# Moving two small shift terms behind the sums of the next row tiles on VectorE, in the first norm

## The chip, the cores and the metric

The kernel runs on one core of a Trainium2 chip. The metric is the device time of one execution in microseconds (us); lower is better. A difference counts as one only above 2%. Engines as the profile names them: PE is TensorE (PEld its weight loads), DVE is VectorE, ACT is ScalarE, POOL is GpSimd, SP issues the loads.

## The reference, cut to what matters

```python
def reference(A_x, A_wqkv, A_wo, B_x, B_w_gate, B_w_up, B_w_down, c, w_mod):
    x = A_x                                            # 1 x 2048 x 1024, bf16
    mod = (silu(c) @ w_mod).reshape(1, 6, 1, 1024)     # sa, ca, ga, sb, cb, gb
    h = layernorm(x) * (1 + ca) + sa                   # the first norm: this case
    x = x + ga * linear_attention(h, A_wqkv, A_wo)
    h = layernorm(x) * (1 + cb) + sb
    return x + gb * swiglu(h, B_w_gate, B_w_up, B_w_down)
```

The change touches `layernorm(x)` for the first four row tiles of 128 rows, so the first 12 us of the kernel. Everything behind is the same in both kernels.

## The kernel before: the parts that matter

Nothing large can start on TensorE until four row tiles are loaded, normalised and transposed. The work is split over all engines. VectorE sums tiles 0, 2 and 3 (two half-sums `bn_stats` and a `bn_aggr` each); ScalarE sums tile 1; POOL computes `rstd` as a power. Tiles 0 and 1 are normalised by ScalarE as `x * rstd + shift`; VectorE forms the shift (`NMR`, a 128x1 value, minus mean times rstd). Tiles 2 and 3 are normalised by VectorE itself. TensorE meanwhile runs dummy matmuls (`warm`), then transposes each tile.

In the traces below VectorE starts its instructions in the order of the program. The loads of x are issued first, one tile each, on one queue:

```python
for st in range(4):
    P.dma("x0_%d" % st, XRES[:, st, :], xv[:, st, :])
# ... then the loads of w_mod and wqkv, in the order of their use

s0_, s2_, s3_ = ln1_stats_ops(0), ln1_stats_ops(2), ln1_stats_ops(3)   # bn_stats, bn_stats, bn_aggr

def act_xn(st, mean):
    P.dve("tensor_scalar", out=NMR[:, st:st + 1], in0=mean, scalar1=RSTD[:, st:st + 1],
          scalar2=-1.0, op0=ALU.mult, op1=ALU.mult)                    # the shift term
    P.act("activation", out=XRES[:, st, :], in_=XRES[:, st, :],
          func=ACT.Identity, scale=RSTD[:, st:st + 1], bias=NMR[:, st:st + 1])

warm(13, bank=3)                 # TensorE: 13 dummies
act_stats(1)                     # ScalarE: sums of tile 1
for f in s0_:
    f()
ln1_rstd1(0)                     # epsilon on VectorE, power on POOL
s2_[0]()
act_xn(0, MV[:, 0, 0:1])
s2_[1]()
tile_transposes(0)
warm(5, bank=3)                  # TensorE: 5 more dummies
act_var(1)
s2_[2]()
P.dve("tensor_scalar", out=VE[:, 2:3], in0=MV[:, 2, 1:2], scalar1=EPS, scalar2=None, op0=ALU.add)
P.pool("tensor_tensor", out=RSTD[:, 1:3], in0=VE[:, 1:3], in1=NEGHALF[:, 0:2], op=ALU.pow)
s3_[0]()
s3_[1]()
act_xn(1, SUMX[:, 1:2])
s3_[2]()
ln1_rstd1(3)
ln1_xn(2)
tile_transposes(2)
mod_sc(WCA, 8, range(2))         # TensorE: first scale columns of the modulation
ln1_xn(3)
fin_ca(0, 2)
tile_transposes(1, 3)
# ... cut: the projection (q_phase_chunk0), which starts with HT[0] and WQK[0]
```

## Time and profile before

| | before |
|---|---|
| time, median of 3 runs | 831.08 us (830.88 to 831.48) |
| span of the profiled execution | 829.0 us |
| TensorE busy | 819.6 us, 99% |
| first weight load of the projection | 11.96 us |

The profile's page of the kernel before, from its parts 1 (busy us of each engine, share of the span, instructions) and 4 (the chain of work that ended last, by engine):

```profile
PE 819.6 (99%) x4005; PEld 379.2 (46%) x4083; DVE 312.5 (38%) x665; ACT 197.5 (24%) x336; POOL 40.4 (5%) x57
...
PE 97%; DVE 2%; issue 1%; ACT 0%; DVEq 0%; ACTq 0%
```

TensorE bounds the kernel, so only time in which TensorE waits in the head, or arrives late there, can matter. The page also counts 4005 matmuls against 4083 weight loads: 78 matmul records are missing from this trace.

The timeline of VectorE in the kernel before (start in us, length in us, instruction, out<-in, count, idle time before it and what ended it):

```profile
5.33 0.69 DVE L176 BATCH_NORM_STATS2 stats<-xres 128x6 f32<-128x512 bf16 x1
6.18 0.21 DVE L176 TENSOR_SCALAR nmr<-mv,rstd 128x1 f32<-128x1 f32 x1 [0.16 <-POOL rstd L176]
6.31 0.68 DVE L176 BATCH_NORM_STATS2 stats<-xres 128x6 f32<-128x512 bf16 x1
6.91 0.20 DVE L176 SCALAR_TENSOR_TENSOR mv<-sumx,sumsq 128x1 f32<-128x1 f32 x1
...
8.71 0.20 DVE L176 TENSOR_SCALAR nmr<-sumx,rstd 128x1 f32<-128x1 f32 x1
8.83 0.21 DVE L176 BATCH_NORM_AGGREGATE mv<-stats 128x2 f32<-128x12 f32 x1
...
10.13 0.55 DVE L176 TENSOR_SCALAR xres<-xres,mv,rstd 128x1024 bf16<-128x1024 bf16 x1 [0.45 <-POOL rstd L176]
```

The two `nmr` lines are the shift terms. The first waits 0.16 us for POOL between the two half-sums of tile 2: that is the wait which the change wants to fill.

ScalarE in the same profile (the `xres` lines normalise tiles 0 and 1):

```profile
6.49 0.19 ACT L176 ACTIVATION_READ_ACCUMULATOR ht<-xres 128x1 f32 x1
6.58 1.23 ACT L176 ACTIVATE xres<-xres,nmr,rstd 128x1024 bf16<-128x1024 bf16 x1
9.01 1.24 ACT L176 ACTIVATE xres<-xres,nmr,rstd 128x1024 bf16<-128x1024 bf16 x1 [1.20 <-DVE nmr L176]
```

And TensorE: transposes of tile 0, five dummies, transposes of tile 2, and those of tiles 1 and 3 (16):

```profile
8.04 0.61 PE L176 MATMUL ps<-ident,xres 128*128 128x128 bf16 x8
8.48 1.24 PE L176 MATMUL ps<-e,ident 128*128 128x512 bf16 x5
9.74 0.62 PE L176 MATMUL ps<-ident,xres 128*128 128x128 bf16 x8
...
10.60 1.15 PE L176 MATMUL ps<-ident,xres 128*128 128x128 bf16 x16
```

### The profile page before, as it was taken

What the parts mean: (1) busy time and instruction counts of PE and PEld (TensorE: products, weight loads), DVE (VectorE), ACT (ScalarE), POOL (GpSimd) and SP (SyncE); (2) the same over time, 40 slices, a digit from 0 to 9 for tenths busy, and PEclk for the clock granted to TensorE, in tenths of its full rate; (3) what the DMA queues carried; (4) which work ended last, traced back from release to release, by engine and by line L of the source; (5) the groups of instructions that cost most, each with busy time, mean ns of one, the idle gap of its engine ahead of it and who ended that gap; (6) DMA issues with size and microseconds to landing.
All of it is one profiled execution on the core that took longest, in us unless ns stands there. A gap on an engine that the chain in (4) does not pass through costs nothing.

```text
span 829.0 us, 9939 instructions
## 1 busy us (share of the span) xinstructions
PE 819.6 (99%) x4005; PEld 379.2 (46%) x4083; DVE 312.5 (38%) x665; ACT 197.5 (24%) x336; POOL 40.4 (5%) x57
## 2 busy tenths in 40 slices
PE   8999999999999999999999999999999999999998
PEld 4544444454444444444444444444444444444444
DVE  5797986756955521121221112122111111221111
ACT  4757641323242111011111101111110111111011
POOL 1010000000130000030000003000000300000000
PEclk9999999999999999999999999999999999999999
DMA  9969655928397995700455571045557004553000
GB/s 320 291 151 232 149 155 172 202 103 304 63 255 231 292 252 153 189 25 18 123 153 154 150 184 33 18 124 153 154 150 189 26 19 123 152 154 86 0 26 26
DMA packets 199245, 119.28 MB, mean 144 GB/s; under 512 B 57880, under 2 KB 182944, under 8 KB 199200
## 3 DMA queue, kind: packets, MB, share of 16 engines
q1 hardware_dynamic: 199184, 118.65, 52.8%
q8 instruction: 32, 0.52, 0.3%
q14 instruction: 13, 0.11, 0.0%
q10 hardware_dynamic: 16, 0.00, 0.0%
HBM read 100.67 MB, written 4.33 MB: 127 GB/s over the span
## 4 chain that ended last, share of the span: by engine, by line
PE 97%; DVE 2%; issue 1%; ACT 0%; DVEq 0%; ACTq 0%
PE ps L176 97%; DVE acc L176 1%; DVE pkt L176 0%; DVE e L176 0%; DVE pqt L176 0%; DVE ht L176 0%; DVE mask L176 0%; ACT e L176 0%; DVE xres L176 0%; DVE zsel L176 0%; DVE modcol L176 0%; DVEq L247 0%; ACTq L247 0%
## 5 line engine op out<-in xcount | busy, mean ns | idle before, releaser
L176 PE MATMUL ps<-h2t,guu 128*128 128x512 bf16 x878 | 210.1, 379 | 0.9
L176 PE MATMUL ps<-h2t,gug 128*128 128x512 bf16 x878 | 209.9, 379 | 0.9
L176 DVE TENSOR_TENSOR at<-sg,ps 128x512 bf16<-128x512 bf16 x112 | 77.0, 688 | 282.7 <-PE ps L176 270.1
L176 ACT ACTIVATE sg<-ps 128x512 bf16<-128x512 f32 x112 | 67.0, 598 | 309.6 <-PE ps L176 298.2
L176 PEld LDWEIGHTS ps<-h2t,guu 128*128 128x128 bf16 x896 | 87.7, 98 | 105.7
L176 PEld LDWEIGHTS ps<-h2t,gug 128*128 128x128 bf16 x896 | 87.6, 98 | 105.5
L176 PE MATMUL ps<-wd_a,at 128*128 128x512 bf16 (+1 forms) x501 | 111.5, 377 | 0.5
L176 PE MATMUL ps<-ht,wqk 128*128 128x512 bf16 x499 | 110.5, 379 | 0.8
L176 PE MATMUL ps<-wd_b,at 128*128 128x512 bf16 (+1 forms) x378 | 84.7, 377 | 0.4
L176 PEld LDWEIGHTS ps<-wd_a,at 128*128 128x128 bf16 x512 | 50.1, 98 | 59.7
L176 DVE TENSOR_TENSOR ut<-att,gb_b 128x512 bf16<-128x512 bf16 (+1 forms) x32 | 14.3, 446 | 166.9 <-ACT att L176 166.9
L176 PEld LDWEIGHTS ps<-ht,wqk 128*128 128x128 bf16 x512 | 49.5, 98 | 58.6 <-DVE biasq L176 0.2
L176 ACT ACTIVATE att<-ps 128x512 bf16<-128x512 f32 (+1 forms) x32 | 17.4, 591 | 182.1 <-PE ps L176 182.1
L176 PEld LDWEIGHTS ps<-wd_b,at 128*128 128x128 bf16 x384 | 37.6, 98 | 44.6
L176 PE MATMUL ps<-pk,xres 128*128 128x512 bf16 x250 | 55.9, 379 | 0.4 <-issue 0.2
L176 PE MATMUL ps<-mw,pqt 128*128 128x512 bf16 x250 | 55.8, 379 | 0.3
L176 POOL TENSOR_SCALAR h2t<-h2t,modcol 128x512 bf16<-128x512 bf16 x32 | 26.5, 844 | 383.0 <-DMA h2t<-xn 383.0
L176 ACT ACTIVATE e<-ps 128x512 bf16<-128x512 f32 x56 | 33.2, 604 | 31.7 <-PE ps L176 20.4
L176 PEld LDWEIGHTS ps<-mw,pqt 128*128 128x128 bf16 x256 | 24.8, 98 | 30.2 <-DVE xres L176 0.4
L176 PEld LDWEIGHTS ps<-pk,xres 128*128 128x128 bf16 x256 | 24.9, 98 | 29.9 <-issue 0.4
L176 ACT ACTIVATE junk<-xres 128x1024 bf16<-128x1024 bf16 x24 | 25.4, 1058 | 35.1 <-DVE xres L176 34.9
L176 DVE SCALAR_TENSOR_TENSOR xres<-ps,xres 128x512 bf16<-128x512 f32 x32 | 21.4, 688 | 12.3 <-PE ps L176 11.5
(107 smaller groups left out, 346.3 us busy)
## 6 DMA issues: line engine op xcount, KB each, us to landing
gug<-in_B_w_gate_dram SPq DMA_DIRECT2D x56, 512.0 KB, 4.1
guu<-in_B_w_up_dram SPq DMA_DIRECT2D x56, 512.0 KB, 5.3
xres<-in_A_x_dram SPq DMA_DIRECT2D x20, 256.0 KB, 7.8
rb<-recip_den SPq DMA_DIRECT2D x8, 512.0 KB, 12.0
stgx<-in_w_mod_dram SPq DMA_DIRECT2D x2, 2048.0 KB, 8.2
wd_a<-in_B_w_down_dram SPq DMA_DIRECT2D x4, 1024.0 KB, 7.8
out_dram<-xres SPq DMA_DIRECT2D x31, 128.0 KB, 1.7
xres<-in_A_x_dram SPq DMA_DIRECT2D x3, 1024.0 KB, 14.2
```

The source lines that it names most:

```text
L176: return getattr(e, method)(**kw)
```

## The change

The intent: the shift of tile 0 needs `rstd` from POOL; by putting the second half-sum of tile 2 ahead of it, VectorE does useful work while POOL finishes. Likewise the shift of tile 1 goes behind the aggregate and the epsilon of tile 3, so that POOL gets tile 3's variance sooner. No instruction is added or removed. The sequence on the other four engines stays the same.

```diff
         ln1_rstd1(0)
         s2_[0]()
+        s2_[1]()
         act_xn(0, MV[:, 0, 0:1])
-        s2_[1]()
         tile_transposes(0)
 ...
         s3_[0]()
         s3_[1]()
-        act_xn(1, SUMX[:, 1:2])
         s3_[2]()
         ln1_rstd1(3)
+        act_xn(1, SUMX[:, 1:2])
         ln1_xn(2)
```

## The prediction

> **What bounds the kernel now.** The page gives TensorE 819.6 us busy of a 829.0 us span (99%), granted clock 1.0; the chain that ended last is 97% PE. The change touches only VectorE's order between 5.3 and 9.7 us, in the first norm. There the timeline shows a tangle: VectorE sums, POOL forms rstd, ScalarE normalises row tiles 0 and 1, VectorE tiles 2 and 3, and TensorE runs 18 dummy matmuls and the transposes. Nothing is added or removed; the comparison of instruction order shows moves on VectorE alone.
>
> **The moves, with durations of the trace.**
> - Shift of tile 0 (0.21 us) goes behind the second half-sum of tile 2 (0.61 us start to start). It starts at 6.18 now, after 0.16 us of waiting for POOL; then at about 6.55. ScalarE's tile 0, at 6.58 now, starts at about 6.86 and ends at 8.08 instead of 7.80. First transpose 8.04 -> about 8.2.
> - The 0.16 us wait goes, because POOL ends (6.14) under the sum: the variance of tile 1 starts at about 6.71 instead of 6.91. All behind it moves 0.2 us earlier: rstd of tiles 1 and 2 ends at about 8.19 (8.39 now).
> - Shift of tile 1 goes behind aggregate and epsilon of tile 3: about 8.95 instead of 8.71, so ScalarE's tile 1 ends at about 10.49 instead of 10.25. In exchange rstd of tile 3 ends at about 9.90 (10.10) and tile 3 is normalised by about 10.48 (10.68).
>
> **How much is critical.** Tile 0's delay is mostly eaten behind the five dummies: they could be followed at 9.56, but the transposes of tile 2 start at 9.74, waiting for VectorE (9.68). Afterwards the dummies end at about 9.7 and tile 2 is ready at about 9.6: a wash. The transposes of tiles 1 and 3 start at 10.60 now, and tile 3 holds the second to 10.735, a loss of 0.08 us. Afterwards both tiles are ready at about 10.5, as TensorE gets there; the last transpose starts at about 11.40 instead of 11.53. Gain there: 0.1 us (-0.05 to 0.2).
>
> I expect even that to be given back. At 20.55 TensorE uses the first shift weights, whose DMA lands at 20.40, and at 24.88 the second, landing at 24.77. DMA share is about 1.0 from 3 to 34 us, and these loads depend on none of the moved work. TensorE arriving earlier waits; only arriving later costs. The remaining 800 us are untouched.
>
> **Prediction.** 831.0 us, 8 times in 10 between 830.3 and 831.8 (before: 831.08). Faster by over 2%: 0.005; within 2%: 0.99; slower by over 2%: 0.005.
>
> **What would show each step.** Timeline, 5 to 12.3 us: no VectorE gap before the first shift term; ScalarE's tile 0 at about 6.86, tile 1 at about 9.25; POOL's second and third power 0.2 us earlier; transposes of tiles 1 and 3 in even 0.056 us steps; first projection matmul at about 12.1 (now 12.20). Shift-weight matmuls at about 20.55 as before, behind the DMA, and the span equal within 0.3 us.
>
> **What would make it wrong.**
> - The Trainium skill, "TensorE: Matmul & The Clock Gate", "What's actually happening", says that the array starts at half rate and that the activity window ending this is free-running, so the moment varies by 0.5 us. The trace agrees on two rates: dummies step by 0.427 us up to 7.70, by 0.216 us from 8.48. A later switch would shift this stretch by tenths, as chance, in either kernel.
> - DMA landings at 20.4 and 24.8 may move by tenths and set the time.
> - Tile 0's delay may not be eaten: +0.2 us.

## The result, and the profile after

| | before | after |
|---|---|---|
| time, median of 6 runs | 831.10 us | 831.06 us (830.66 to 831.47) |
| ratio | | 0.9999, 95% interval 0.9986 to 1.0012 |
| span of the profiled execution | 829.0 us | 829.4 us |
| first weight load of the projection | 11.96 us | 12.41 us |

A ratio is the mean time of one kernel's fast runs over that of the other's of the same rounds, so it isn't quite the ratio of the medians. All runs were on one core; the three jobs of the experiments ran on three different chips. Granted clock 1.000 means full clock from its first rise on.

The time is the same. But the head of the profile looks quite unlike what I predicted. VectorE after:

```profile
5.94 1.29 DVE L176 BATCH_NORM_STATS2 stats<-xres 128x6 f32<-128x512 bf16 x2 [0.58 <-DMA xres<-in_A_x_dram]
7.14 0.20 DVE L176 TENSOR_SCALAR nmr<-mv,rstd 128x1 f32<-128x1 f32 x1
7.25 0.21 DVE L176 SCALAR_TENSOR_TENSOR mv<-sumx,sumsq 128x1 f32<-128x1 f32 x1
...
9.18 0.21 DVE L176 BATCH_NORM_AGGREGATE mv<-stats 128x2 f32<-128x12 f32 x1
...
9.50 0.20 DVE L176 TENSOR_SCALAR nmr<-sumx,rstd 128x1 f32<-128x1 f32 x1
9.62 1.18 DVE L176 TENSOR_SCALAR xres<-xres,mv,rstd 128x1024 bf16<-128x1024 bf16 x2
```

The wait for POOL is gone, as intended. In its place stands a wait of 0.58 us for the load of tile 2, which landed at 5.92 here, and both half-sums of that tile now stand ahead of the first shift. The shift starts at 7.14, where I had said 6.55. ScalarE and TensorE follow:

```profile
7.46 1.24 ACT L176 ACTIVATE xres<-xres,nmr,rstd 128x1024 bf16<-128x1024 bf16 x1 [0.86 <-DVE mv L176]
9.80 1.24 ACT L176 ACTIVATE xres<-xres,nmr,rstd 128x1024 bf16<-128x1024 bf16 x1 [1.10 <-DVE nmr L176]
```

```profile
8.76 0.62 PE L176 MATMUL ps<-ident,xres 128*128 128x128 bf16 x8 [0.42 <-ACT xres L176]
9.21 1.24 PE L176 MATMUL ps<-e,ident 128*128 128x512 bf16 x5
10.29 0.61 PE L176 MATMUL ps<-ident,xres 128*128 128x128 bf16 x8
...
11.14 1.05 PE L176 MATMUL ps<-ident,xres 128*128 128x128 bf16 x16
```

The first transpose is 0.72 us later than before; those of tile 2 are 0.55 us later, and the projection's first weights 0.45 us. The chain that ended last, for the first 13 us of the kernel after (start, length, what; five pieces ahead of the load of tile 2 are cut), says why:

```profile
...
1.71 4.21 DMA xres<-in_A_x_dram
5.92 0.02 issue
5.94 1.29 DVE stats L176 x2
7.22 0.11 DVE nmr L176
7.34 0.14 DVE mv L176
7.47 1.23 ACT xres L176
8.71 0.05 issue
8.76 4.27 PE ps L176 x71
```

(The profile infers releasers: it names `mv`, the next VectorE instruction, between the shift and ScalarE, though ScalarE needs the shift alone, which ended at 7.34.) The head of the kernel after is one chain without slack: the landing of tile 2, its two half-sums, the shift of tile 0 (which needs nothing of tile 2), ScalarE, then TensorE without a pause. The question is whether the order or the landing took the 0.45 us, and why the time doesn't show it.

### The profile page after: what moved, and what is told of

The parts are those of the page before. It is cut to its first block, busy times and chain, and to the rows that moved or that the text cites. A ratio compares the mean times of both kernels' runs of the same rounds, so it can differ in the third digit from the quotient of the medians.

```text
span 829.4 us, 10017 instructions
## 1 busy us (share of the span) xinstructions
PE 824.0 (99%) x4083; PEld 378.4 (46%) x4083; DVE 312.0 (38%) x665; ACT 197.6 (24%) x336; POOL 39.8 (5%) x57
## 3 DMA queue, kind: packets, MB, share of 16 engines
HBM read 100.67 MB, written 4.33 MB: 127 GB/s over the span
## 4 chain that ended last, share of the span: by engine, by line
PE 99%; DMA 1%; DVE 0%; ACT 0%; SPq 0%; issue 0%
PE ps L176 99%; DMA xres<-in_A_x_dram 1%; DVE stats L176 0%; ACT xres L176 0%; SPq L176 0%; DVE xres L176 0%; DVE mv L176 0%; DVE nmr L176 0%
## 5 line engine op out<-in xcount | busy, mean ns | idle before, releaser
L176 ACT ACTIVATE e<-ps 128x512 bf16<-128x512 f32 x56 | 33.1, 603 | 31.7 <-PE ps L176 20.5
```

The costliest lines, as they stand in the source:

```text
L176: return getattr(e, method)(**kw)
```

## The experiments

Two theories went into the first four runs. W: the two orders are about a wash, and the difference between the two profiles is the landing of tile 2, which differs from execution to execution. R: the new order itself costs the 0.45 us.

### Controls: both kernels once more

No edit; each is profiled and timed in 5 rounds.

> The kernel before, unchanged, as a control. Theory W (the two orders are a wash, and what differs between the two profiles is the landing of row tile 2 of x: 4.96 us in the profile of before, 5.92 in that of after): the landing varies from execution to execution in this kernel too, ratio 1.000 within 0.001, and where tile 2 lands at about 5.9 the first shift still starts at about 6.5 and ScalarE's tile 0 at about 6.95. Rival R (the new order itself brings the late landing or costs 0.45 us): tile 2 always lands at about 5.0 here, and the span is 829.0.

> The changed kernel, unchanged, as a control. W: in a profile where tile 2 lands before 5.3 the first shift starts at about 6.55, ScalarE's tile 0 at about 6.86, and the projection's first matmul at about 12.1; with a late landing as in the first profile 7.14, 7.46 and 12.4. Ratio to before 1.000 within 0.001. R: first shift at about 7.1 again, span 829.4, ratio 1.0005.

### Each half of the change alone

```diff
 # only0: the first half of the change
         s2_[0]()
-        act_xn(0, MV[:, 0, 0:1])
         s2_[1]()
+        act_xn(0, MV[:, 0, 0:1])
```

```diff
 # only1: the second half of the change
-        act_xn(1, SUMX[:, 1:2])
         s3_[2]()
         ln1_rstd1(3)
+        act_xn(1, SUMX[:, 1:2])
```

> Only tile 0's shift moved. W: first shift 6.55 (tile 2 early) or 7.14 (late), second shift straight behind tile 3's sums, 0.2 us earlier than with both moved, so ScalarE's tile 1 ends 0.4 us earlier than tile 3 is ready; the time is 831.1 within 0.4. R: the loss of 0.45 us comes from this half: ratio 1.0005.

> Only tile 1's shift moved. W: first shift at 6.18 (early) or about 6.5 (late), first transpose at 8.04 to 8.2; second shift 0.35 us later than in before, tile 3 ready 0.12 us earlier; the transposes of tiles 1 and 3 start within 0.1 us of 10.6. Ratio 1.000 within 0.001. R: no loss here, all of it in the other half.

**Measured.** The times of all four agree with the kernel before (before in this job: 831.42 us median of 9):

| run | median, us | range | ratio, 95% interval |
|---|---|---|---|
| b_again | 831.83 | 830.99 to 832.09 | 1.0004 (0.9990 to 1.0017) |
| a_again | 831.29 | 830.99 to 831.62 | 0.9998 (0.9986 to 1.0011) |
| only0 | 831.44 | 831.25 to 833.40 | 1.0006 (0.9994 to 1.0019) |
| only1 | 831.41 | 830.93 to 831.63 | 0.9999 (0.9987 to 1.0012) |

The control of before already shows that its first profile was a lucky one. VectorE in b_again:

```profile
5.81 0.69 DVE L176 BATCH_NORM_STATS2 stats<-xres 128x6 f32<-128x512 bf16 x1 [0.49 <-DMA xres<-in_A_x_dram]
6.42 0.20 DVE L176 TENSOR_SCALAR nmr<-mv,rstd 128x1 f32<-128x1 f32 x1
6.53 0.68 DVE L176 BATCH_NORM_STATS2 stats<-xres 128x6 f32<-128x512 bf16 x1
```

Here, too, VectorE waits for the load and not for POOL. Tile 2 landed at 5.79 (b_again), 5.92 (after), 6.08 (a_again), 6.01 (only0) and 5.67 us (only1), and only in the profile that I predicted from at 4.96. (A landing is the moment at which the load's semaphore reaches its value in the trace.) So I subtract the landing of tile 2 from every mark. All numbers are us after that landing:

| mark | b_again: none moved | only1: tile 1's moved | only0: tile 0's moved | after: both | a_again: both |
|---|---|---|---|---|---|
| first shift starts | 0.633 | 0.635 | 1.227 | 1.225 | 1.226 |
| first transpose | 2.247 | 2.249 | 2.840 | 2.840 | 2.840 |
| tile 1 ready (ScalarE) | 4.684 | 5.129 | 4.685 | 5.124 | 5.122 |
| tile 3 ready (VectorE) | 5.120 | 4.889 | 5.118 | 4.881 | 4.884 |
| transposes of tile 2 start | 4.180 | 4.303 | 4.376 | 4.375 | 4.376 |
| projection's first weight load | 6.405 | 6.468 | 6.496 | 6.496 | 6.496 |

**What follows.** The two columns of the changed kernel agree to 0.01 us (and so, further down, do the same marks of b_late and b_clean with those of b_again, on other chips), so the landing is the origin of this stretch and the rest is arithmetic.
- Moving tile 0's shift delays it by 0.59 us, one half-sum, and the first transpose by the same 0.59 us. It brings nothing forward: tiles 1 and 3 are ready when they were. The wait for POOL was not there to be filled.
- Moving tile 1's shift delays tile 1 by 0.44 us and makes tile 3 0.23 us earlier. The later of the two is ready at 5.12 to 5.13 in every column: a wash. But it also starts tile 2's transposes 0.12 us later (4.303 against 4.180), because the shift now stands directly ahead of tile 2's normalisation, and alone it costs 0.06 us at the projection (6.468 against 6.405). In the old order the shift starts before the sums' recorded end and fills the time in which the aggregate waits for them (8.71, 8.80 and 8.83 in the first profile); in the new order it stands behind the aggregate and the epsilon.
- So POOL does not get tile 3's variance sooner, as the change intended: POOL's third power starts 3.75 us after the landing in every column. Tile 3 is earlier because that power is shorter, 0.56 us instead of 0.79. This is so in all eight profiles with tile 1's shift moved, against all six with it in its old place. Here it is in the kernel before, then in the kernel after:

```profile
9.31 0.79 POOL L176 TENSOR_TENSOR rstd<-ve,neghalf 128x1 f32<-128x1 f32 x1 [0.92 <-DVE ve L176]
9.66 0.56 POOL L176 TENSOR_TENSOR rstd<-ve,neghalf 128x1 f32<-128x1 f32 x1 [0.92 <-DVE ve L176]
```

What shortens it isn't shown. One difference at its start: in the old order VectorE has been normalising tile 2 for 0.16 us by then, in the new one for 0.04 us.

- Of the 0.59 us, 0.09 us is left at the projection (6.496 against 6.405), because in the old order TensorE waited for tiles 2 and 3 behind the five dummies. The second half adds nothing to that: only0 and the whole change both stand at 6.496.

Of the 0.45 us between the two first profiles, then, 0.09 us is the order's, measured at equal landing. With the landing of the profile after, the old order would have loaded the first weights at 5.915 + 6.405 = 12.32 us (an estimate from the table), so 0.36 us is the landing's. R falls; W holds but for those 0.09 us. My expectation for only1, transposes of tiles 1 and 3 within 0.1 us of 10.6, failed (10.85), because it still took the lucky landing for granted.

**Where the 0.09 us and the landings go.** TensorE doesn't use the shift weights (`wsa`) before about 20.5 us. In b_again it got there early and waited; the line of weight loads on PE:

```profile
21.02 0.47 PEld L176 LDWEIGHTS ps<-siluc,wsa 128*128 128x128 bf16 x16 [0.57 <-DMA wsa<-in_w_mod_dram]
```

This load landed at 20.98 there. By 28 us b_again is behind the kernel after: its first exponential starts at 28.30, that of after at 28.02, although its projection began 0.22 us earlier (12.19 against 12.41). In only1 the load landed at 20.01 and TensorE went through without waiting. What the head wins or loses is thus hidden in some executions and shown in others, by tenths, below the spread of the time.

### Tile 2's load from ScalarE's queue

To take the landing away as a cause, tile 2's load goes to another queue, where it was meant to come first.

```diff
+        P.dma("x0_2", XRES[:, 2, :], xv[:, 2, :], queue="act")
-        for st in range(4):
+        for st in (0, 1, 3):
             P.dma("x0_%d" % st, XRES[:, st, :], xv[:, st, :])
```

> The order of before, with tile 2 of x loaded first, from ScalarE's queue. Theory L (the sums of tile 2 wait for its load, which lands at 5.7 to 6.1 us in five of six profiles and at 4.96 in the one that I predicted from): tile 2 lands before 5.3, VectorE has no gap before its first sum, first shift at 6.18 as in the first profile, first projection weights loaded at about 11.96. Rival M (the reorder costs the same whenever tile 2 lands): nothing to tell here, it is the partner of the next run. Time 831.1 within 0.5.

> The order of after, same early load. L: the timeline that I predicted comes true: first shift at about 6.55, ScalarE's tile 0 from 6.86 to 8.08, first transpose at about 8.2, last transpose at about 11.4, first projection weights at about 11.85, so 0.1 us earlier than in the partner. M: first transpose at about 8.8, first projection weights 0.3 to 0.4 us later than the partner's (12.3). Time 831.1 within 0.5 in both.

**Measured.** The premise was met only in part. On ScalarE's queue the load stands behind that of `c`, so that it was issued at 1.40 us, after those of tiles 0 and 1 (0.79 and 1.25 in b_early) and only 0.3 us earlier than otherwise (1.70). Tile 2 landed at 5.49 and 5.45, and tile 1 half a us later than in the other runs (4.86 and 4.84 against 4.15 to 4.33). The Trainium skill, "DMA: Bandwidth & Descriptors", "Queues, rings and completion order", says that the queue of SP and that of ScalarE are rings on the same 16 DMA engines, which take turns between them packet by packet; tile 1's delay agrees with that. With tile 1 late, ScalarE's own sums hold tile 0: it starts at 7.12 in b_early and at 7.10 in a_early, though the shifts start at 6.12 and 6.68 (b_early, then a_early):

```profile
7.12 1.22 ACT L176 ACTIVATE xres<-xres,nmr,rstd 128x1024 bf16<-128x1024 bf16 x1
7.10 1.22 ACT L176 ACTIVATE xres<-xres,nmr,rstd 128x1024 bf16<-128x1024 bf16 x1
```

The first transposes then agree (8.40 and 8.38) and the projection's first weights differ by 0.04 us (12.32 and 12.36). So the order costs nothing at the first transpose when something else holds tile 0 for as long; rival M, a cost whatever the landing, falls. It was the late tile 1 that hid the cost here, though, and not an early tile 2. The timeline that I had predicted did not come true here either. Times: 831.59 us (ratio 1.0002) and 831.27 us (ratio 0.9999), against 831.68 us.

### Tile 2's load behind tile 3's

```diff
-        for st in range(4):
+        for st in (0, 1, 3, 2):
             P.dma("x0_%d" % st, XRES[:, st, :], xv[:, st, :])
```

> The order of before, with tile 2 loaded behind tile 3, so that it lands at about 6.7. L: first shift 0.62 us behind the landing or so (about 7.3), second sum after it; first projection weights at about 12.9, later than the control's 12.19 by 0.7.

> The order of after, same late load. L: first shift 1.22 us behind the landing (about 7.9), first transpose at about 9.5, first projection weights 0.3 to 0.4 us later than in the partner, about 13.2. M says the same difference, so this pair gives the slope (how much of the landing's delay comes through in each order) and the early pair decides.

**Measured.** Tile 2 landed at 6.62 and 6.82. The first shift starts 0.634 us (old order) and 1.226 us (new order) behind it, as in the table. In b_late the projection's first weights load at 13.03, again 6.405 us behind the landing. But in a_late they load at 14.90, not at 13.3 as the table would have it, and the time is 833.71 us (b_late 831.83; one run each). TensorE in a_late, and busy times in two stretches of 3.41 us (the columns: stretch, its length, busy us with instruction counts for PE, PEld, DVE, ACT and POOL, granted clock, DMA share, GB/s):

```profile
2.64 4.68 PE L176 MATMUL ps<-e,ident 128*128 128x512 bf16 x13
9.66 1.03 PE L176 MATMUL ps<-ident,xres 128*128 128x128 bf16 x8 [2.34 <-ACT xres L176]
10.48 2.34 PE L176 MATMUL ps<-e,ident 128*128 128x512 bf16 x5
```

```profile
6.11:9.52 3.41, 1.21 (x6) 0.35 (x4) 2.61 (x9) 1.69 (x3) 0.58 (x1) 1.00 1.06 370
9.53:12.94 3.41, 3.28 (x17) 1.91 (x17) 2.01 (x6) 1.31 (x2) 0.67 (x2) 0.50 1.09 362
```

Its TensorE was granted half clock from 9.53 to 12.94, and the five dummies took 2.34 us instead of 1.24. Before that it had idled for 2.34 us between the dummies and the first transpose, and was busy for 1.21 us of the preceding 3.41. The Trainium skill, "TensorE: Matmul & The Clock Gate", "What's actually happening", tells of an activity window of 3.41 us that runs free, and of a return to half clock after an idle one. The clock's record agrees with the length (3.41 us for each piece). It differs in that the window before the fall wasn't idle.

### Is it the idle gap, and is it chance?

```diff
 # a_late2: a_late unchanged, 3 rounds.   a_late_warm: a_late with
-        warm(13, bank=3)
+        warm(20, bank=3)
```

> The same kernel as a_late, which took 833.7 us: its TensorE was granted half clock for 3.41 us from 9.53, after an idle gap of about 2.3 us before the first transpose. Theory C (chance of the phase: the gap falls into one clock window or is split over two): several of these runs are at about 832.0, others at 833.5 to 834. Rival S: each execution loses the clock, all at 833.5 to 834.

> The same late load and order, with 20 instead of 13 dummy matmuls ahead of the first transposes. If the idle gap of TensorE lets the clock fall, then here no run is above 832.5, the clock is 1.0 from its first rise on, and the projection starts at about 13.2 instead of 14.9. If the clock fell for another reason, half of the runs or more stay at 833.5.

**Measured.** Four runs of a_late2: 833.98 us at clock 0.998, and 831.76, 831.60 and 831.84 us, all at 1.000. So it isn't every execution (rival S falls): with a_late, two executions of five lost the clock, and paid about 2.1 us (the mean of the two, 833.85, less the mean of the other three, 831.73; an estimate from few runs). In the profile of a_late2 the clock fell in the same way after a gap of 2.18 us. In both profiles the 13 dummies had ended early, at 7.32 and 7.62 us (8.20 in the kernel before), which lengthened the gap. How the gap lies to the clock's windows, the reason that theory C gives, isn't shown: no undisturbed execution of a_late was profiled. With seven more dummies all four runs were at 1.000, the gap before the first transpose was 0.64 us, and the projection's first weights loaded at 13.43, 6.499 us behind the landing, as in the table. That the gap is the cause is supported by this, not proven: at two in five, four good runs come by chance about once in eight (0.6 to the fourth). One expectation failed: a run was at 832.81 us with the clock at 1.000, which the clock cannot explain; that stays open.

This bears on the change. One of the five runs of only0 took 833.40 us, and its mean clock was 0.998, as in the disturbed runs of a_late. It wasn't profiled, so where the clock fell isn't shown. None of the other 15 timed runs of the changed kernel and of only0 had it, nor any run of the old order with unchanged loads for which the clock was recorded.

### No weight load until tile 2 has landed

A second attempt at an early landing: the weights' loads compete with x, so hold them back.

```diff
-        for st in range(4):
-            P.dma("x0_%d" % st, XRES[:, st, :], xv[:, st, :])
+        x0 = [P.dma("x0_%d" % st, XRES[:, st, :], xv[:, st, :]) for st in range(4)]
+        P.wait_for("sp", [x0[2]])
```

> The order of before; no weight load is issued until tile 2 of x has landed, so that nothing competes with the four tiles (the weights come later, and the whole kernel may be 1 to 2 us slower: only the stretch up to the transposes counts). Theory L: tiles 1 and 2 land at about 4.3 and 5.0, and the first profile's timeline returns: first shift 6.18, ScalarE's tile 0 at 6.58, first transpose at 7.9 to 8.04, those of tile 2 at 9.74.

> The order of after, same loads: the premises of my prediction, made true. L: first shift 6.55, ScalarE's tile 0 6.86 to 8.08, first transpose at about 8.2, those of tile 2 at about 9.7, last transpose at about 11.4, so no loss against the partner (unless a weight's landing holds both). M (the reorder costs whatever the landing): first transpose at about 8.8 and those of tile 2 at about 10.3.

**Measured.** The premise failed again: tile 2 landed at 5.69 and 5.89 with no weights in flight. So the weights' loads are not what makes it late. The marks behind the landing are as in the table (first shift in a_clean 1.226 us, first transpose 2.838 us; in b_clean 0.634 and 2.249 us), and the first transposes are at 7.94 and 8.73. From there on the held-back scale weights (landed at 10.76 and 11.05 us) limit both kernels, and the whole is slower by 1.3 to 1.6 us (832.66 and 832.95 us, one run each, against 831.40), as expected. No run here made an early landing in the new order, so the timeline that I predicted was never put to the test; that stays open.

## Why the prediction was right, and which steps of it were not

The predicted 831.0 us and its range, 830.3 to 831.8, held: 831.06 us. The argument that carried it was sound: no work is added, what is at stake is tenths of a us in the head, and 800 us of TensorE's work behind are untouched. The hit says nothing for the single steps, though: they move tenths, and the range would have held whichever way they went. Point by point:

- **"after 0.16 us of waiting for POOL", "The 0.16 us wait goes"**: this is the step that failed. The wait was real in the one profile that I read, where tile 2 landed at 4.96. In all other executions with unchanged loads that were profiled, the landing was 5.67 to 6.08, so that the first half-sum ended at 6.39 to 6.80, after POOL (5.98 to 6.13), and VectorE waited 0.29 to 0.77 us for the load. There was no such wait to fill, so "all behind it moves 0.2 us earlier" did not happen for tiles 1 and 2 (only tile 3 came earlier, by 0.23 us, through the other half of the change and POOL's shorter power).
- **First transpose 8.04 to 8.2**: mis-sized. I had 0.16 us, because ScalarE's own accumulator read and the last cold dummies hid part of the delay. Measured at equal landing it is the whole half-sum, 0.59 us (2.840 less 2.247).
- **Shift of tile 1 against rstd of tile 3**: the trade is there, but not by the mechanism that I gave. Tile 1 is later by 0.44 us (I had 0.24, with the 0.2 us gain that did not come). Tile 3 is earlier by 0.23 us (I had 0.20), which is luck: I had "POOL's second and third power 0.2 us earlier", and both start where they do in the old order, 2.12 and 3.75 us after the landing; the third one is shorter. I had the later of the two tiles ready 0.19 us sooner (10.49 instead of 10.68); it is ready at the same time.
- **"Tile 0's delay is mostly eaten behind the five dummies"**: right. 0.50 of the 0.59 us are eaten, 0.40 behind the five dummies and 0.10 at the wait for tile 3.
- **Even 0.056 us steps in the transposes of tiles 1 and 3**: right; the step of 0.135 us is gone in the profile after.
- **"Gain there: 0.1 us (-0.05 to 0.2)"**: wrong in sign, a loss of 0.09 us at the projection's start. The mark that I used for it, a first projection matmul at 12.20, was the second one, as the first record is missing.
- **Given back at the shift weights**: the wait is real where TensorE arrives early (b_again, 0.57 us). In the profile after, TensorE came late and did not wait at all. Whether it waits is decided by a landing that ranges from 20.0 to 21.0 us in the profiles with unchanged loads.

## What to carry to other kernels

A landing time read from one profile is one draw, and an order tuned to it is tuned to chance: profile the kernel a few times before moving an instruction over a wait. Measure marks from the event that starts the chain (here the landing of a tile); differences of 0.1 us become legible that neither the clock time nor the span can show. And don't put a short instruction that releases another engine behind work that waits for a load it doesn't need: in this stretch that cost 0.59 us at the next engine, most of it hidden by luck of the slack behind it.

## What the Trainium skill lacked or had wrong

- "TensorE: Matmul & The Clock Gate", section "What's actually happening": it gives an idle window as the condition for falling back to half clock. Here the clock fell after windows of 3.41 us in which TensorE was busy for about a third (1.21 us in a_late, 1.23 us in a_late2), with gaps of 2.34 and 2.18 us; a full idle window wasn't needed. It stayed at full clock where 2.31 us of the 3.41 from its rise were busy (b_late, 7.33 to 10.74). The window's length agreed.
- "DMA: Bandwidth & Descriptors": no page tells of the hole in the first loads of an execution. Four equal loads of 256 KB were issued 0.46 us apart on one queue. The second landed 0.62 to 0.78 us after the first, but the third 1.1 to 1.8 us after the second, in eleven of twelve such profiles. In the twelfth, the one that I predicted from, it took 0.65 us, and the hole of 1.80 us came before the fourth. It isn't the weights' loads (1.51 us in b_clean and 1.74 us in a_clean without them); its cause is open.
- No page has a duration for `bn_stats`, or the start-to-start times of it and of 128x1 instructions beside it: a half-sum of 128x512 bf16 takes 0.69 us and the next independent one starts 0.61 us after it; a 128x1 shift starts 0.11 to 0.13 us before its successor; an instruction that depends on the one just ahead starts 0.03 us after that one's end.
